# Adding u back without TensorE for 22 more token groups: VectorE transposes, a DRAM round trip and an add

## The chip, the cores and the metric

One core of a Trainium2 chip runs the whole program. The metric is the device time of one execution in microseconds; lower is better.

## The reference

The input is `x` of 8 batches, 3136 tokens and 256 channels. First a global filter along the tokens, by FFT; then a low-rank token mixer; then an MLP over the channels with a residual:

```
X = rfft(x, axis=1);  Y = X * (filt_r + 1j*filt_i);  y = irfft(Y)
h = (y^T @ U) @ V                 # U: 3136 x 32, V: 32 x 3136
u = y + h^T
out = u + relu(u @ w_ch1) @ w_ch2 # 256 -> 1024 -> 256
```

The output is float32; the kernel computes in float16 with float32 accumulation.

## The kernel before, in words

The 3136 tokens of a batch are taken as 49 x 64, and the transforms are matmuls with constant matrices. For each batch there are five stages, each a Python generator that issues a piece of its work at each `next`:

- `f1` (or `f1_turned` for batches 0 and 1): the first transform. `load_x` brings `x` in four blocks per batch, issued on GpSimd's queue (line 128). TensorE multiplies (L250), ScalarE copies the result into a tile with the tag `asb` (L255), and SyncE's queue stores it to DRAM (L257, L258).
- `mid`: loads what `f1` stored into `a2` tiles (L331, SyncE's queue; one load of 512 KB covers eight frequencies), second transform `pz` (L384, TensorE), product with the filter on VectorE (`uv`, L392, L396, L397), back transform `pe` (L345), a copy by ScalarE, and a store to DRAM (`ct2`, L364, SyncE's queue). A batch has 13 items of this kind; `pe` of an item comes three items later.
- `load_e2` reads `ct2` back into the rows of `eb` (L416), in three parts and two halves of 32 columns, 256 KB each.
- `rank`: the low-rank term (L423 and on), written into rows of `eb` by VectorE (L438).
- `s4`: the last transform (`pu`, L456), 16 items, the first eight from the first half of `eb`, copied by VectorE and ScalarE into `ut`. `ut` holds u with channels on the partitions.

The MLP works on 49 groups of 512 tokens, eight steps to a group: step t of group n issues `mm1` for it (L488, ReLU by ScalarE L491 into `h16`) and `mm2` for group n-1 (L544). `mm2` puts tokens on the partitions, so u must be turned before it can be added. There are two ways:

- `residual`: two matmuls with the identity for each 128 tokens (L536) add u to the accumulator `pc` in PSUM; VectorE then copies `pc` to `och` (L556). A group has eight such matmuls, in four pairs.
- `turn_u`, for groups from `FIRST_TURNED` = 37 on: two VectorE transposes of 32 x 32 blocks (L515) into a tile `tu`, four stores of 64 KB to DRAM (L520) and one load of 256 KB into `tur` (L524), both on SyncE's queue; VectorE then adds `pc` and `tur` into `och` (L552). The generator has four pieces: first transpose, second transpose, stores, load.

Every half group (steps t = 3 and t = 7 of `mm2`) ends in such a copy or add; at t = 7 GpSimd's queue issues the output of 512 KB (L561).

The order of the work is written out by hand: `plan[s]` lists which generators are advanced at the end of step s, of 392 steps. `S[b]` is the step at which the first group that reaches into batch b starts (0, 48, 96, 144, 192, 240, 288, 336). In the loop over b, `a` = S[b-1], `z` = S[b], and `e` = z-20 (z-17 for b = 1, z-22 for b = 6 and 7): `mid` of batch b is dealt over the steps from a-5 to e, its loads follow at e-5, e-4 and e+1, `rank` from e, `s4` from e+8 to z-2; at the same time `x` of batch b+1 is loaded and `f1` of it is dealt from a+10 to z-20 (a+21 to z-13 for b = 1). In those steps the MLP is working on batch b-1. Each engine, and each DMA queue, takes its instructions in this order and waits where its data or its buffer is not ready. A transfer that waits for a buffer holds up all that stand behind it on the same queue.

Of the kernel before, what the change touches and what calls it, by code (L numbers as in the profile page):

```python
# [10 lines left out]
F16 = mybir.dt.float16  # L11
# [7 lines left out]
DM = 256  # L19
# [3 lines left out]
NG = NB * SEQ // GT  # L23
FIRST_TURNED = 37
# [56 lines left out]
def kernel(  # L81
# [27 lines left out]
    sb = ctx.enter_context(tc.tile_pool(name="sb", bufs=1))  # L109
    ps = ctx.enter_context(tc.tile_pool(name="ps", bufs=2, space=bass.MemoryType.PSUM))  # L110

    def bank(tag, name, dtype=F32):

        return ps.tile([128, 512 if dtype == F32 else 1024], dtype, tag=tag, bufs=4 if tag == "z" else 2, name=name)

    def dram(t, off, dims):
        return bass.AP(tensor=t, offset=off, ap=[list(d) for d in dims])
# [5 lines left out]
    xt = {}  # L123

    def load_x(b, c):
        t = sb.tile([98, 8 * DM], F16, tag="x", bufs=4, name="x")
        for a, n in ((0, 96), (96, 2)) if b == 0 else ((0, 98),):
            nc.gpsimd.dma_start(t[a:a + n], dram(x.tensor, (b * SEQ + 8 * c + 32 * a) * DM, [[32 * DM, n], [1, 8 * DM]]))
        xt[b, c] = t
# [10 lines left out]
    for c in range(4):  # L140
        load_x(0, c)
# [64 lines left out]
    tu = eb[0:RANK, 0:12, :].rearrange("p r d -> p (r d)")  # L206
# [34 lines left out]
    def f1(b):  # L241
        for c in range(4):
            t = xt[b, c].rearrange("p (j d) -> p j d", d=DM)
            asb = sb.tile([98, 8, DM], F16, tag="asb", bufs=4, name="asb")
            for half in range(2):
                for i in range(2):
                    pf = bank("z", "pf")
                    for s in range(2):
                        j = 4 * half + 2 * i + s
                        nc.tensor.matmul(pf[0:98, 256 * s:256 * s + 256],  # L250
                                         ws[:, (8 * c + j) * 98:(8 * c + j + 1) * 98], t[:, j, :],
                                         start=(s == 0), stop=True, skip_group_check=True)
                    dst = asb[:, 4 * half + 2 * i:4 * half + 2 * i + 2, :]
                    src = pf[0:98].rearrange("p (j d) -> p j d", d=DM)
                    nc.scalar.copy(dst, src)  # L255
                    if half and i:
                        nc.sync.dma_start(dram(ct1[b], 8 * c * 96 * DM, [[DM, 96], [96 * DM, 8], [1, DM]]), asb[0:96])  # L257
                        nc.sync.dma_start(dram(ct0[b], 8 * c * DM, [[32 * DM, 2], [1, 8 * DM]]),  # L258
                                          asb[96:98].rearrange("p j d -> p (j d)"))
                    yield  # L260
# [151 lines left out]
    def load_e2(b, part, hs=(0, 1)):  # L412

        n = 12 if (b, part) == (0, 2) else 16
        for h in hs:
            nc.sync.dma_start(eb[32 + part:32 + 4 * n:4, 32 * h:32 * h + 32, :].rearrange("p (q r) d -> p q (r d)", r=8),  # L416
                              dram(ct2[b][part], 8 * h * DM, [[NR * DM, n], [16 * DM, 4], [1, 8 * DM]]))
# [61 lines left out]
    groups = [Group(n) for n in range(NG)]  # L479

    def utv(b):
        return ut[b].rearrange("p h q r -> p h (q r)")
# [11 lines left out]


    def turned(gr):
        return gr.n >= FIRST_TURNED

    def turn_u(gr):

        t = sb.tile([128, 4, 4, 2, 32], F16, tag="asb", bufs=4, name="tu")
        for dh in range(2):
            for b, t0, o, n in gr.seg:
                j, z = o // 32, (o + n) // 32
                while j < z:

                    k = min(z, j + 4 - j % 4) if j % 4 or z - j < 4 else z - z % 4
                    src = utv(b)[:, dh, t0 + 32 * j - o:t0 + 32 * k - o]
                    if k - j < 4:
                        dst = t[:, j % 4:j % 4 + k - j, j // 4, dh, :]  # L510
                        src = src.rearrange("p (c e) -> p c e", e=32)
                    else:
                        dst = t[:, :, j // 4:k // 4, dh, :].rearrange("p c g e -> p g c e")
                        src = src.rearrange("p (g c e) -> p g c e", c=4, e=32)
                    nc.vector.transpose(dst, src)  # L515
                    j = k
            yield
        td = nc.dram_tensor(f"tu_{gr.n}", (128, 4 * DM), F16, kind="Internal")
        for a in range(4):
            nc.sync.dma_start(dram(td, DM * a, [[4 * DM, 32], [128 * DM, 4], [1, DM]]),  # L520
                              t[32 * a:32 * a + 32].rearrange("i c g h e -> i c (g h e)"))
        yield
        gr.tu = sb.tile([128, 4, 4, 2, 32], F16, tag="x", bufs=4, name="tur")
        nc.sync.dma_start(gr.tu.rearrange("p a g h e -> p (a g h e)"), td.ap())  # L524
        yield

# [11 lines left out]
    def mm2(gr, t):  # L538
        i, half = t // 2, t % 2
        if t % 4 == 0:  # L540
            gr.pc = bank("o", "pc")
        o = gr.pc[:, 256 * (i % 2):256 * (i % 2) + 256]
        for tt in range(4 * half, 4 * half + 4):
            nc.tensor.matmul(o, gr.h[tt][:, 128 * i:128 * i + 128], w2sb[:, tt, :],  # L544
                             start=(tt == 0), stop=(tt == 7 and turned(gr)), skip_group_check=True)
        if half and not turned(gr):
            residual(gr, o, i)
        if t % 4 == 3:
            if t == 3:
                gr.och = sb.tile([128, 4, DM], F32, tag="och", bufs=2, name="och")  # L550
            if turned(gr):
                nc.vector.tensor_add(gr.och[:, i - 1:i + 1, :].rearrange("p g (h a e) -> p (g h) a e", h=2, a=4),  # L552
                                     gr.pc.rearrange("p (f a e) -> p f a e", f=4, a=4),
                                     gr.tu[:, :, i - 1:i + 1].rearrange("p a g h e -> p (g h) a e"))
            else:
                nc.vector.tensor_copy(gr.och[:, i - 1:i + 1, :], gr.pc.rearrange("p (j d) -> p j d", d=DM))  # L556
            if gr.n == NG - 1:
                nc.sync.dma_start(dram(out.tensor, (gr.n * GT + 128 * (i - 1)) * DM, [[DM, 128], [128 * DM, 2], [1, DM]]),
                                  gr.och[:, i - 1:i + 1, :])
            elif t == 7:  # L560
                nc.gpsimd.dma_start(dram(out.tensor, gr.n * GT * DM, [[DM, 128], [128 * DM, 4], [1, DM]]), gr.och)  # L561
# [3 lines left out]
    plan = [[] for _ in range(8 * NG)]  # L565

    def deal(gen, count, a, z):
        for i in range(count):
            plan[max(0, int(a + i * (z - a) / count))].append(gen)

    def later_x(b, c):
        load_x(b, c)
        yield

    f1s = [f1(b) if b > 1 else f1_turned(b) for b in range(NB)]
    mids = [mid(0, "o")] + [mid(b) for b in range(1, NB)]
    ranks = [rank(b) for b in range(NB)]
    s4s = [s4(b) for b in range(NB)]
    turns = [turn_u(gr) for gr in groups]

    u_hat()
# [4 lines left out]
    for i in range(16):  # L586
# [3 lines left out]
        next(f1s[0])  # L590
    nc.gpsimd.dma_start(sv[32:97], sv_d.rearrange("k (r q) -> k r q", q=NQ))
    load_x(1, 0)
    nc.gpsimd.dma_start(w1sb, moe_w_ch1.rearrange("(h dd) c -> dd h c", h=2))
    spread_filters(2)
# [29 lines left out]
    for _ in s4s[0]:  # L624
        pass

    def loads(b, part):
        load_e2(b, part)
        yield

    for b in range(1, NB):
        a, z = S[b - 1], S[b]
        e = z - (17 if b == 1 else 20 if b < 6 else 22)
        deal(mids[b], 13, a + {1: 8, 2: -3}.get(b, -5), e - 4)
        deal(mids[b], 4, e - 4, e)
        for p, at in enumerate((e - 5, e - 4, e + 1)):
            plan[at].append(loads(b, p))
        deal(ranks[b], 6, e, e + 6)
        deal(s4s[b], 16, e + 8, z - 2)
        if b == 1:  # L640
            deal(f1s[1], 12, 1, 8)
        if b + 1 < NB:
            for c in range(4):
                plan[a + (9 + 2 * c if b == 1 else 1 + 4 * c)].append(later_x(b + 1, c))
            deal(f1s[b + 1], 16, a + (21 if b == 1 else 10), z - (13 if b == 1 else 20))

    for gr in groups:
        if turned(gr):
            for i in range(4):
                plan[8 * gr.n + (0, 1, 2, 5)[i]].append(turns[gr.n])  # L650
    for n, gr in enumerate(groups):
        for t in range(8):
            mm1(gr, t)
# [36 lines left out]
```

## Time and profile before

| what | value |
|---|---|
| three runs | 517.74, 514.62, 516.92 us; median 516.92 |
| the profiled execution | 516.43 us, of which the span of the program is 514.6 us |
| TensorE busy | 490.5 us (95%), granted clock 0.995 |
| VectorE / ScalarE / GpSimd busy | 366.2 / 377.1 / 80.6 us |
| moved by DMA | 94.52 MB |
| L536, matmuls with the identity | 302 |
| L515, transposes on VectorE | 28 |

A line of the groups in the profile reads: source line, engine, operation, result and sources, shape, count, then busy time and mean duration of one in nanoseconds, then the idle time of the engine just before these instructions and what ended it. A line of the order of time reads: start and length in microseconds, engine, line, operation, and in brackets the idle time before it with its releaser. A line of a stretch gives the busy time of TensorE, of its weight loads, of VectorE, ScalarE and GpSimd, then the granted clock, the busy share of the DMA engines and the GB/s.

### The profile page before, as it was taken

The numbers are of one execution on the slowest core, as the hardware profiler recorded it, in microseconds if no ns is written. First come the engines' busy times: TensorE is split into PE (matmuls) and PEld (weight loads), VectorE is DVE, ScalarE is ACT, GpSimd is POOL, SyncE is SP. The second block draws the span as 40 slices with busy tenths as digits, with TensorE's granted clock in tenths as the row PEclk, the third lists the DMA queues.
The fourth block names the chain that finished last, engine by engine and source line by source line (L and its number), as shares of the span: only waits on it lengthen the run. The fifth ranks groups of instructions, "written<-read, shape, count | busy, mean of one in ns | idle before, by whom it ended". The sixth has DMA issues, their size and how long they took to land.

```text
span 514.6 us, 11909 instructions
## 1 busy us (share of the span) xinstructions
PE 490.5 (95%) x4754; PEld 349.6 (68%) x4754; DVE 366.2 (71%) x497; ACT 377.1 (73%) x704; POOL 80.6 (16%) x122
## 2 busy tenths in 40 slices
PE   3887899999999999999999999999999998999996
PEld 3645566776767777777767777777677765676665
DVE  5886599579847986679747986679846997853332
ACT  6874778867986689667986689667886676666663
POOL 6662010002001110002001110002001000011110
PEclk9998999999999999999999999999999999999999
DMA  8987926957877286837877286837877136644454
GB/s 187 175 206 174 181 74 172 281 171 176 216 229 251 69 186 190 298 130 177 213 227 254 69 185 202 262 156 184 218 228 240 65 126 206 212 153 149 126 162 163
DMA packets 76016, 94.52 MB, mean 184 GB/s; under 512 B 5795, under 2 KB 58979, under 8 KB 75960
## 3 DMA queue, kind: packets, MB, share of 16 engines
q1 hardware_dynamic: 61256, 52.17, 33.9%
q0 software_dynamic: 14704, 41.58, 31.4%
q8 instruction: 37, 0.61, 0.5%
q14 instruction: 19, 0.16, 0.1%
HBM read 58.35 MB, written 50.92 MB: 212 GB/s over the span
## 4 chain that ended last, share of the span: by engine, by line
PE 81%; DVE 8%; DMA 4%; issue 1%; ACT 1%; SPq 0%; POOL 0%; DVEq 0%; POOLq 0%
PE pc L544 31%; PE phh L488 30%; DVE uv L392 5%; PE pu L456 5%; PE pf L250 4%; PE pe L345 4%; PE pz L384 3%; PE pc L536 3%; DMA w2sb<-in_moe_w_ch_dram 2%; PE ph L423 1%; DVE uv L397 1%; DMA eb<-ct 1%; DVE uv L396 1%; DMA ct<-e 1%; DVE och L556 1%
## 5 line engine op out<-in xcount | busy, mean ns | idle before, releaser
L491 ACT ACTIVATE h<-phh 128x512 f16<-128x512 f32 x392 | 235.9, 603 | 83.2 <-PE phh L488 81.7
L544 PE MATMUL pc<-w2sb,h 128*128 128x256 f16 x1568 | 233.7, 272 | 1.2 <-DMA w2sb<-in_moe_w_ch_dram 1.2
L488 PE MATMUL phh<-ut,w1sb 128*128 128x512 f16 (+7 forms) x896 | 233.3, 352 | 0.4 <-DVE ut L463 0.4
L544 PEld LDWEIGHTS <-h 128*128 128x128 f16 x1568 | 151.7, 97 | 91.8 <-issue 1.5
L392 DVE TENSOR_TENSOR uv<-pz,fab 128x1024 f16<-128x1024 f32 (+1 forms) x104 | 120.6, 1177 | 12.5 <-PE pz L384 10.5
L561 POOL DMA_DIRECT2D out_dram<-och x48 | 39.1, 814 | 402.0 <-DVE och L556 318.8
L488 PEld LDWEIGHTS <-w1sb 128*128 128x128 f16 x896 | 78.9, 97 | 19.8 <-issue 1.5
L556 DVE COPY och<-pc 128x512 f32<-128x512 f32 x74 | 51.0, 689 | 44.4 <-PE pc L536 43.5
L355 ACT CAST e<-pe 128x512 f16<-128x512 f32 x96 | 56.6, 591 | 21.0 <-PE pe L345 20.2
L463 DVE CAST ut<-pu 128x392 f16<-128x392 f32 x92 | 48.5, 557 | 17.9 <-PE pu L456 16.0
L255 ACT CAST asb<-pf 98x512 f16<-98x512 f32 x96 | 57.3, 599 | 0.2
L438 DVE COPY eb<-h 32x4096 f16<-32x4096 f16 x32 | 38.2, 1232 | 14.2 <-ACT h L435 14.2
L552 DVE TENSOR_TENSOR och<-pc,tur 128x512 f32<-128x512 f32 x24 | 16.5, 689 | 39.8 <-PE pc L544 37.3
L345 PE MATMUL pe<-uv,m 128*128 128x512 f16 (+1 forms) x117 | 41.3, 371 | 3.6 <-DVE uv L392 1.5
L456 PE MATMUL pu<-sv,eb 97*128 97x49 f16 x1024 | 40.5, 187 | 3.3 <-DMA eb<-ct 3.1
L456 PEld LDWEIGHTS <-eb 97*128 97x128 f16 x1024 | 37.7, 98 | 4.8 <-DVE eb L438 3.4
L536 PE MATMUL pc<-idn,ut 128*128 128x128 f16 (+1 forms) x302 | 40.8, 219 | 0.0
L384 PE MATMUL pz<-a,m 128*128 128x512 f16 x96 | 36.2, 379 | 1.1 <-DVE a L311 1.0
L250 PE MATMUL pf<-x,ws 98*98 98x256 f16 x192 | 36.6, 273 | 0.0
L396 DVE TENSOR_TENSOR uv<-uv 64x1024 f16<-64x1024 f16 (+1 forms) x49 | 30.9, 630 | 1.7
L536 PEld LDWEIGHTS <-ut 128*128 128x128 f16 (+1 forms) x302 | 28.8, 98 | 3.9 <-issue 0.6
L397 DVE TENSOR_TENSOR uv<-uv 64x1024 f16<-64x1024 f16 (+1 forms) x49 | 30.7, 627 | 0.7
(80 smaller groups left out, 264.9 us busy)
## 6 DMA issues: line engine op xcount, KB each, us to landing
out_dram<-och POOLq DMA_DIRECT2D x48, 512.0 KB, 4.4
ct<-e SPq DMA_DIRECT2D x47, 256.0 KB
eb<-ct SPq DMA_DIRECT2D x46, 256.0 KB
x<-in_x_dram POOLq DMA_DIRECT2D x28, 392.0 KB, 7.8
ct<-asb SPq DMA_DIRECT2D x24, 384.0 KB
a<-ct SPq DMA_DIRECT2D x18, 512.0 KB
tu<-tu SPq DMA_DIRECT2D x48, 64.0 KB
tur<-tu SPq DMA_DIRECT2D x12, 256.0 KB
```

Source lines behind the costliest of these rows:

```text
L250: nc.tensor.matmul(pf[0:98, 256 * s:256 * s + 256], ws[:, (8 * c + j) * 98:(8 * c + j + 1) * 98], t[:, j, :], start=(s == 0), stop=True, s ...
L255: nc.scalar.copy(dst, src)
L345: nc.tensor.matmul(pe[:, 0:n], w, uv[:, f, o:o + n], start=(f == 0), stop=(b > 0 or f == 1))
L355: nc.scalar.copy(t[:, 2 * (i % 2):2 * (i % 2) + 2, :].rearrange("p k d -> p (k d)"), pe)
L384: nc.tensor.matmul(pz, a2m, src[:, k:k + 2, :].rearrange("p k d -> p (k d)"), start=True, stop=True)
L392: nc.vector.tensor_mul(uv[:, :, o:o + n], zin, fin)
L456: nc.tensor.matmul(pu[:, NQ * i:NQ * i + NQ], eb[:, 8 * n + i, d], sv[:, 8 * g + i, :], start=(i == 0), stop=True, skip_group_check=True)
L488: nc.tensor.matmul(ph[:, o:o + n], w1sb[:, dh, 128 * t:128 * t + 128], utv(b)[:, dh, t0:t0 + n], start=(dh == 0), stop=(dh == 1), skip_gro ...
L491: nc.scalar.activation(h, ph, RELU)
L536: nc.tensor.matmul(d, w, idn, start=False, stop=(dh == 1), skip_group_check=True)
L544: nc.tensor.matmul(o, gr.h[tt][:, 128 * i:128 * i + 128], w2sb[:, tt, :], start=(tt == 0), stop=(tt == 7 and turned(gr)), skip_group_check ...
L556: nc.vector.tensor_copy(gr.och[:, i - 1:i + 1, :], gr.pc.rearrange("p (j d) -> p j d", d=DM))
```

## The change

The last four groups of each of the batches 1 to 5 (two of batch 0), counted from 0 as the batches in the MLP, take the second way too: the groups 4 and 5, 8 to 11, 14 to 17, 20 to 23, 26 to 29 and 32 to 35. Their pieces are put at steps of their own relative to z and e. `tu` and `tur` get two buffers of their own instead of sharing those of `asb` and `x`, which go from four to three each. Three of the first eight `x` blocks are put in `asb` buffers. The fourth `x` block of a batch is loaded five steps later (twelve for batch 2). The rows of `eb` are loaded half by half: the first halves at e-5, e-4 and e+1, the second halves of all three parts at e+2.

```diff
     def load_x(b, c):
-        t = sb.tile([98, 8 * DM], F16, tag="x", bufs=4, name="x")
+        tag = "asb" if (b, c) in ((0, 3), (1, 0), (1, 1)) else "x"
+        t = sb.tile([98, 8 * DM], F16, tag=tag, bufs=3, name="x")
...
-            asb = sb.tile([98, 8, DM], F16, tag="asb", bufs=4, name="asb")
+            asb = sb.tile([98, 8, DM], F16, tag="asb", bufs=3, name="asb")
...
     def turned(gr):
-        return gr.n >= FIRST_TURNED
+        return gr.n >= FIRST_TURNED or gr.n in turn_at
...
-        t = sb.tile([128, 4, 4, 2, 32], F16, tag="asb", bufs=4, name="tu")
+        t = sb.tile([128, 4, 4, 2, 32], F16, tag="tu", bufs=2, name="tu")
...
-        gr.tu = sb.tile([128, 4, 4, 2, 32], F16, tag="x", bufs=4, name="tur")
+        gr.tu = sb.tile([128, 4, 4, 2, 32], F16, tag="tur", bufs=2, name="tur")
...
-    def loads(b, part):
-        load_e2(b, part)
+    def loads(b, parts, h):
+        for part in parts:
+            load_e2(b, part, [h])
         yield
+    turn_at = {n: [8 * n + i for i in (0, 1, 2, 5)] for n in range(FIRST_TURNED, NG)}
...
-        for p, at in enumerate((e - 5, e - 4, e + 1)):
-            plan[at].append(loads(b, p))
+        for at, parts, h in ((e - 5, [0], 0), (e - 4, [1], 0), (e + 1, [2], 0), (e + 2, range(3), 1)):
+            plan[at].append(loads(b, parts, h))
+        if z < 8 * FIRST_TURNED:
+            if b > 1:
+                turn_at[z // 8 - 4] = [z - 37, z - 35, z - 33, z - 29]
+                turn_at[z // 8 - 3] = [z - 31, z - 29, z - 27, z - 23]
+            turn_at[z // 8 - 2] = [e - 3, e - 2, e + 3, e + 7]
+            turn_at[z // 8 - 1] = [e - 1, e, e + 5, z - 8]
...
-                plan[a + (9 + 2 * c if b == 1 else 1 + 4 * c)].append(later_x(b + 1, c))
+                plan[a + (9 + 2 * c + 12 * (c > 2) if b == 1 else 1 + 4 * c + 5 * (c > 2))].append(later_x(b + 1, c))
...
-    for gr in groups:
-        if turned(gr):
-            for i in range(4):
-                plan[8 * gr.n + (0, 1, 2, 5)[i]].append(turns[gr.n])
+    for n, at in turn_at.items():
+        for i in at:
+            plan[i].append(turns[n])
```

## The prediction

> **What bounds the kernel now.** I read the page first, then TensorE's waits, then TensorE, VectorE and SyncE in order of time at one batch boundary (batch 3 to 4), then stretches.
>
> ```profile
> span 514.6 us, 11909 instructions
> PE 490.5 (95%) x4754; PEld 349.6 (68%) x4754; DVE 366.2 (71%) x497; ACT 377.1 (73%) x704; POOL 80.6 (16%) x122
> PE   3887899999999999999999999999999998999996
> DVE  5886599579847986679747986679846997853332
> DMA  8987926957877286837877286837877136644454
> L536 PE MATMUL pc<-idn,ut 128*128 128x128 f16 (+1 forms) x302 | 40.8, 219 | 0.0
> ```
>
> TensorE has a 9 in every slice from 64 us to 424 us, and after 60 us its waits for other work come to 2.5 us in all. So time on TensorE is time of the kernel, unless taking work off it starves it. The loss would come from VectorE, which is full in some slices and half idle in others, or from the transfers, which go in bursts.
>
> **Part 1: the residual matmuls removed.** `turned` becomes true for 22 more groups: 4 and 5 of batch 0, then the last four of each of batches 1 to 5 (8-11, 14-17, 20-23, 26-29, 32-35; groups that straddle two batches stay). Each loses 4 pairs of L536. Matmuls overlap, so the 219 ns is not their price; the distance between starts is:
>
> ```profile
> 220.27 0.27 PE L536 MATMUL pc<-idn,ut 128*128 128x128 f16 x2
> 220.38 0.58 PE L456 MATMUL pu<-sv,eb 97*128 97x49 f16 x16
> ...
> 225.75 0.38 PE L384 MATMUL pz<-a,m 128*128 128x512 f16 x1
> ```
>
> A pair holds TensorE from 220.27 to 220.38, 0.11 us. 22 groups x 4 pairs x 0.11 = **9.7 us off**. The order of the built program shows it: 352 fewer rows on TensorE, 176 weight loads and 176 matmuls.
>
> **Part 2: VectorE's new work.** Each group adds two transposes and turns two copies into adds.
>
> ```profile
> L515 DVE STREAM_TRANSPOSE tu<-ut 128x512 f16<-128x512 f16 x22 | 14.5, 688 | 0.1
> L552 DVE TENSOR_TENSOR och<-pc,tur 128x512 f32<-128x512 f32 x24 | 16.5, 689 | 39.8 <-PE pc L544 37.3 <-DMA tur<-tu 2.5
> L556 DVE COPY och<-pc 128x512 f32<-128x512 f32 x74 | 51.0, 689 | 44.4 <-PE pc L536 43.5
> ```
>
> Add and copy cost the same 689 ns. The transposes are 44 x 0.69 = 30 us, hidden where VectorE has idle time. The first four of a batch (steps z-37, z-35, z-31, z-29) fall, in batch 4's `mid`, into about 246 to 257 us:
>
> ```profile
> 246.00:250.00 4.00, 4.00 (x34) 2.98 (x33) 2.88 (x4) 3.69 (x8) 0.00 (x0) 1.00 0.96 182
> 250.00:254.00 4.00, 4.00 (x30) 2.68 (x29) 3.05 (x4) 3.68 (x8) 0.79 (x1) 1.00 0.78 232
> 254.00:258.00 4.00, 4.00 (x32) 2.92 (x31) 3.32 (x5) 3.49 (x8) 0.00 (x0) 1.00 0.79 243
> ```
>
> VectorE's column (the third engine) leaves 1.12 + 0.95 + 0.68 = 2.75 us; four transposes take 2.75. It just fits, and the next 4 us hold 1.07 more. The other four (around e) fall into 262 to 270 us, where it is idle 6.1 of 8. Batch 6 has less room: 2.0 us idle in 362 to 374, so 0.8 us of lag reaches the end of its `mid`. If the cover is gone, the price has a precedent in batch 7, where two turned groups already meet a `mid`:
>
> ```profile
> 432.12 0.39 PE L345 MATMUL pe<-uv,m 128*128 128x512 f16 x1 [1.33 <-DVE uv L397]
> ```
>
> So the bounds are 0 and 1.3 us in each of five `mid`s, 0 to 6.5. I take 0.4 in all, half of batch 6's lag: four of five stretches fit.
>
> **Part 3: SyncE's queue, and what waits in it.** Each group adds four stores of 64 KB and one load of 256 KB, 22 x 0.52 = 11.5 MB. Per batch 2.1 MB; in the tail, where only such stores, loads and the output move, 20 us carry 3.2 MB at a busy share of 0.49, 3.1 us per MB, so a batch gains 6.5 us of transfer in its 58 us: room on average (share about 0.7), not in every burst. The added wait that matters is the last group's `tur` load, at step z-8. `tur` has two buffers, so this load waits for the second add of the group two before, at step z-9. Queued behind it on SyncE are the loads of `a2` for the next `mid` (L331), which TensorE needs at step z-5. Before, they went out early:
>
> ```profile
> 212.78 1.16 SPq L416 DMA_DIRECT2D eb<-ct  x2
> 214.04 0.54 SPq L331 DMA_DIRECT2D a<-ct  x1
> ...
> 220.58 0.69 DVE L556 COPY och<-pc 128x512 f32<-128x512 f32 x1 [0.42 <-PE pc L536]
> ```
>
> They leave at 214.04, 11.7 us before the matmul at 225.75. Afterwards they leave when the add that stands where this copy stands has ended, 221.27. From there to 225.75 is 4.48 us (163.50 to 168.0 and 279.30 to 283.8 in other batches: the same), less two removed pairs, 4.26. In it a `tur` load (256 KB) and the first `a2` load (512 KB) must land. The nearest row is the last `tur` load:
>
> ```profile
> 506.45 0.34 SPq L524 DMA_DIRECT2D tur<-tu  x1
> ...
> 509.11 0.69 DVE L552 TENSOR_TENSOR och<-pc,tur 128x512 f32<-128x512 f32 x1 [1.34 <-DMA tur<-tu]
> ```
>
> 2.66 us from issue to use on quiet queues. 512 KB more at the 293 GB/s of 213 to 222 us, or at peaks of 380, are 1.8 or 1.4 us: 4.1 to 4.5 us. The group's output (512 KB, other queue) leaves at the same moment and can put up to 1.8 us between. So a stall of 0 to 2.0 us per boundary; I take 0.6, the output costing a third of its bytes. Boundaries where this happens: into batches 3 to 7, five (group 5's load finds a fresh buffer). **Plus 3.0 us**, bounds 0 and 10.
>
> The Trainium skill gives another price: DMA: Bandwidth & Descriptors, section Anatomy of one DMA, fits a transfer on the GpSimd path as 2.0 us plus its bytes at 436 GB/s. The 2.66 us of the 256 KB load agree with its 2.6; by it the 768 KB would take 3.8 us, as an estimate, less than the 4.26 allowed, and the stall would be nothing. The same page (section Rules for kernel authors) says that below 64 KB a transfer is mostly overhead; the four 64 KB stores stand at that edge, and no run here shows one large store instead.
>
> **Part 4: the rest.** (a) Row loads by halves: the same six transfers per batch; the later halves follow 0.6 us apart from 213 us, 1 MB and an output at 293 GB/s land by about 219, and the first use is the ninth `s4` item at 222.86. Nothing. In batch 7 two of these loads now stand ahead of group 39's `tur` load, whose add already waited 1.13 us at 446.30; 1.2 us of issue more, of which I count 0.4 (bounds 0 and 2). (b) The fourth `x` load goes out behind the output at step a+15, about 193.3 in batch 4's loading, and is needed at 201.93. The first `x` load behind an output landed after 5.7 to 6.3 us, a second one after up to 9.1: I take 0, bounds 0 and 0.5 in each of five. Batch 2's is needed at 95.14 and leaves at 87.3. (c) Three asb buffers: `f1`'s fourth block meets a store issued 11 us before. 0. (d) The prologue's x loads wait less; TensorE's wait there for the second weight was 1.2 us, so 0, bounds -1.2 and +1.2.
>
> **Sum.** The profiled execution took 516.43 (span 514.6 and 1.8 around it), 0.5 below the median of 516.92. 516.43 - 9.7 + 0.4 + 3.0 + 0.4 = 510.5; from the median 511.0. I predict **510.8**. The terms' ends give 505.5 and 528; as not all go one way, the forecast's own range is 508 to 513.5.
>
> **Rivals.**
> *No stall at all.* The `a2` loads land in time; 516.4 - 9.7 = 506.7. For it: the quiet landing lies at the limit and 222 to 226 us show a transfer share of only 0.36. Against: that stretch now holds what was moved there. The skill's fit ends here.
> *VectorE becomes the bound.* Every one of the five `mid`s pays batch 7's 1.3 us and the boundary still pays: 510.5 + 6 = 516. For it: 2.75 us of work into 2.75 us of gaps. Against: after its `mid` VectorE has a gap of 4 us and more in each batch, and TensorE uses a product three items later.
> *`a2` loads much too late: slower.* One mechanism: SyncE held at the `tur` load, then the first `a2` load landing like an `x` load on busy queues, 7.8 us instead of the 3.9 left after its issue: 3.9 x 5 = 19.5 on top of 506.7 is 526. It ends slower than before once a landing takes more than 5.8 us. For it: eight stores and four row loads stand ahead on the queue, and the last of them may hold SyncE beyond the add. Against: the queue drained at 300 to 380 GB/s there.
> That the edit does not do what it says is excluded by the 176 missing matmuls.
>
> **Numbers.** Forecast 0.44, no stall 0.24, VectorE 0.15, late loads 0.17. A measurement tells 1%, about 5.2 us, from nothing: 511.75 is the border. Of the forecast 0.32 lies below it, 0.12 above; no stall is faster; VectorE same; of late loads 0.15 slower, 0.02 same. Faster 0.56, same 0.29, slower 0.15. Range: 506 to 521, leaving out about 0.05 below and 0.15 above.
>
> **What would show it.** Right: L536 at 126 matmuls; TensorE's waits name a `pz` matmul waiting for an `a2` load five times, about 0.6 us each; the `a2` loads issued within 1 us of the add at z-9; transposes 72 in all, and VectorE busy about 396 us. Wrong: `pe` waiting for VectorE in every `mid` (the VectorE rival), `pf` waiting for `x` (then part 4b was mis-sized), or `pz` waits of several us (late loads); no waits and 507 would say that my landing price was too high.

## The result, and the profile after

The changed kernel is slower: a median of 540.5 us (533.0 to 547.7, six runs) against 516.0 (514.4 to 519.0) of the kernel before on the same chip, a ratio of **1.037 [1.033, 1.041]**. The profiled execution took 542.6 us and is one of the longer ones, while the ratio rests on the shorter ones (533 to 538); readings of single waits below are therefore on the high side by some us in all. Line numbers of the changed kernel are higher by 2 than those of before (`pz` L386, `pu` L458, `turn_u` L517 to L526, `residual` L538, `mm2` L546, add L554).

The page of the changed kernel, its span, its engines, and three of its rows in 40 slices:

```profile
span 540.9 us, 11742 instructions
PE 490.7 (91%) x4578; PEld 343.2 (63%) x4578; DVE 392.0 (72%) x541; ACT 375.8 (69%) x704; POOL 80.8 (15%) x122
PE   4887899979997899799999899889999798999996
PEclk9998999979999899989999999989999899999999
DMA  9987727948798387885897588976897435834444
```

TensorE executes 176 matmuls less and is still busy for 490.7 us. Its row, which was 9 everywhere from 64 to 424 us, has dents at every batch boundary, and the row of the granted clock has dents in the same slices or the next at five of the six. (A boundary here is the stretch in which `mid` of one batch ends, its `s4` begins with `pu`, and `mid` of the next begins with `pz`; it is named by the z of the loop over b, 48 to 288.)

Its groups by line, those that the change touches:

```profile
L554 DVE TENSOR_TENSOR och<-pc,tur 128x512 f32<-128x512 f32 x68 | 46.8, 689 | 64.8 <-PE pc L546 55.8 <-DMA tur<-tu 7.9
L517 DVE STREAM_TRANSPOSE tu<-ut 128x512 f16<-128x512 f16 (+2 forms) x72 | 45.8, 662 | 4.7 <-DMA tu<-tu 4.2
L538 PE MATMUL pc<-idn,ut 128*128 128x128 f16 (+1 forms) x126 | 16.6, 220 | 0.0
```

126 matmuls with the identity are left, and VectorE does 72 transposes and 68 adds: the edit does what it says.

TensorE's waits (engine, result, line, what it waited for; us in total, times, longest):

```profile
PE pz L386 <- DMA a<-ct: 11.8, 5, 3.4
PE pu L458 <- DMA eb<-ct: 9.2, 4, 3.4
...
PE pu L458 <- issue: 3.5, 2, 3.3
PE pu L458 <- DVE ut L465: 2.7, 2, 1.6
PE pe L347 <- DVE uv L399: 1.5, 1, 1.5
```

Two loads cost most: `a2` of the next `mid`, and `eb`, the rows for `s4`. Of the 9.2 us for `eb`, one wait of 3.4 us ends at 43.9 us, in the prologue, where the kernel before has the like of it:

```profile
PE pu L456 <- DMA eb<-ct: 3.1, 1, 3.1
```

At the boundaries `eb` costs 5.8 us under its name. The 3.3 us under "issue" are read as a wait for `eb` as well: at the boundary at z = 144 `pu` starts 3.33 us after the loads of `eb` leave, and where the trace names the wait it was 3.9, 3.9 and 4.1 us. ScalarE's copy of the last `mid` item at that boundary, SyncE's queue, and the two matmuls, in three views:

```profile
217.25 0.63 ACT L357 CAST e<-pe 128x512 f16<-128x512 f32 x1
```

```profile
220.32 0.34 SPq L526 DMA_DIRECT2D tur<-tu  x1
220.71 0.51 SPq L366 DMA_DIRECT2D ct<-e  x1
...
226.87 2.44 SPq L418 DMA_DIRECT2D eb<-ct  x4
229.41 4.45 SPq L522 DMA_DIRECT2D tu<-tu  x8
234.47 2.02 SPq L526 DMA_DIRECT2D tur<-tu  x2
236.56 0.42 SPq L333 DMA_DIRECT2D a<-ct  x1
```

```profile
230.20 0.82 PE L458 MATMUL pu<-sv,eb 97*128 97x49 f16 x16 [3.26 <-issue]
...
241.56 0.39 PE L386 MATMUL pz<-a,m 128*128 128x512 f16 x1 [1.02 <-DVE ut L465]
```

The copy has ended at 217.88. The store of its result (`ct2`) leaves 2.83 us later, because a `tur` load stands ahead of it and waits for its own four stores. That is the common case: from 60 to 430 us SyncE's queue stood 21.8 us at such loads (L526) for their stores, and 3.2 us for an add.

```profile
SPq L526 <- DMA tu<-tu: 21.8, 17, 4.3
SPq L526 <- DVE och L554: 3.2, 3, 2.0
```

The store lands at 226.87, when the loads of `eb` leave; 3.33 us later the first of them lets `pu` start. Behind `eb` SyncE issues eight stores for 4.45 us, then two `tur` loads, then `a2` at 236.56. The other boundaries look alike, with the delay divided between `pu` and `pz` in other parts: 1.6 + 2.4, 2.2 + 3.4, 3.3 + 1.0, 1.0 + 2.1, 2.6 + 0.8 and 0 + 3.2 us (z = 48, 96, 144, 192, 240, 288), 23.5 in all. Two of these, the 1.6 at z = 48 and the 1.0 at z = 144, the trace puts down to VectorE's copy of `pu` (L465) and not to a load.

At five of the six boundaries a second loss follows. Stretches of the changed kernel around a `pz` wait that ends at 177.99 (TensorE, weight loads, VectorE, ScalarE, GpSimd, then granted clock, DMA share, GB/s):

```profile
174.00:178.00 4.00, 0.60 (x13) 0.46 (x11) 1.16 (x2) 0.62 (x2) 0.00 (x0) 1.00 1.00 355
178.00:180.00 2.00, 2.00 (x22) 1.45 (x23) 1.27 (x2) 0.60 (x1) 0.00 (x0) 0.69 0.43 174
180.00:182.00 2.00, 2.00 (x19) 1.20 (x16) 0.99 (x2) 0.60 (x1) 0.00 (x0) 0.50 0.00 0
182.00:184.00 2.00, 2.00 (x20) 1.33 (x18) 1.42 (x2) 1.18 (x3) 0.00 (x0) 0.96 0.00 0
```

While TensorE is idle, the DMA engines are full (share 1.00); when the data is there, TensorE soon runs at half its clock, for 3.41 us (178.76 to 182.17). There are five such spells after 60 us, one of them twice as long; the kernel before has none there:

```profile
113.91:120.74 6.83, 5.40 (x20) 2.74 (x21) 2.62 (x4) 1.20 (x3) 0.35 (x1) 0.50 0.43 155
178.76:182.17 3.41, 3.41 (x36) 2.42 (x34) 1.92 (x3) 1.20 (x2) 0.00 (x0) 0.50 0.05 19
229.96:233.37 3.41, 3.17 (x39) 2.35 (x40) 1.31 (x3) 0.60 (x1) 0.00 (x0) 0.50 0.92 279
352.84:356.25 3.41, 3.41 (x32) 2.00 (x29) 1.58 (x3) 1.08 (x2) 0.00 (x0) 0.50 0.77 231
424.52:427.93 3.41, 3.41 (x27) 2.13 (x26) 1.68 (x2) 1.19 (x2) 0.00 (x0) 0.50 0.25 101
```

TensorE worked 18.8 us in them, which costs 9.4 us.

### The profile page after: what moved, and what is told of

Its sections match the earlier page's. It is cut to its first block, busy times and chain, and to the rows that moved or that the text cites. A ratio compares the mean times of both kernels' runs of the same rounds, so it can differ in the third digit from the quotient of the medians.

```text
span 540.9 us, 11742 instructions
## 1 busy us (share of the span) xinstructions
PE 490.7 (91%) x4578; PEld 343.2 (63%) x4578; DVE 392.0 (72%) x541; ACT 375.8 (69%) x704; POOL 80.8 (15%) x122
## 4 chain that ended last, share of the span: by engine, by line
PE 56%; DMA 22%; issue 10%; DVE 6%; ACT 2%; POOL 2%; SPq 1%; POOLq 0%; DVEq 0%
PE pc L546 21%; PE phh L490 21%; DMA x<-in_x_dram 6%; DMA ct<-e 6%; DMA a<-ct 5%; PE pu L458 4%; DVE uv L394 3%; DMA eb<-ct 3%; PE pf L252 3%; PE pe L347 2%; PE pz L386 2%; DMA tur<-tu 1%; POOL x L130 1%; SPq L418 1%; ACT e L357 1%
## 5 line engine op out<-in xcount | busy, mean ns | idle before, releaser
L546 PE MATMUL pc<-w2sb,h 128*128 128x256 f16 x1568 | 237.5, 276 | 0.8 <-DMA w2sb<-in_moe_w_ch_dram 0.8
L490 PE MATMUL phh<-ut,w1sb 128*128 128x512 f16 (+7 forms) x896 | 237.1, 357 | 0.4 <-DVE ut L465 0.4
L546 PEld LDWEIGHTS <-h 128*128 128x128 f16 x1568 | 153.5, 99 | 94.9 <-issue 5.8
L554 DVE TENSOR_TENSOR och<-pc,tur 128x512 f32<-128x512 f32 x68 | 46.8, 689 | 64.8 <-PE pc L546 55.8
L490 PEld LDWEIGHTS <-w1sb 128*128 128x128 f16 x896 | 80.6, 98 | 20.7 <-issue 2.1
L357 ACT CAST e<-pe 128x512 f16<-128x512 f32 x96 | 56.6, 591 | 18.7 <-PE pe L347 18.0
L465 DVE CAST ut<-pu 128x392 f16<-128x392 f32 x92 | 48.3, 559 | 28.1 <-PE pu L458 25.8
L458 PE MATMUL pu<-sv,eb 97*128 97x49 f16 x1024 | 42.2, 190 | 15.5 <-DMA eb<-ct 9.2
L458 PEld LDWEIGHTS <-eb 97*128 97x128 f16 x1024 | 40.3, 100 | 19.6 <-issue 10.4
L386 PE MATMUL pz<-a,m 128*128 128x512 f16 x96 | 36.8, 385 | 14.3 <-DMA a<-ct 11.8
L517 DVE STREAM_TRANSPOSE tu<-ut 128x512 f16<-128x512 f16 (+2 forms) x72 | 45.8, 662 | 4.7 <-DMA tu<-tu 4.2
L399 DVE TENSOR_TENSOR uv<-uv 64x1024 f16<-64x1024 f16 (+1 forms) x49 | 30.7, 627 | 0.7
L252 PEld LDWEIGHTS <-ws 98*98 98x98 f16 x192 | 22.4, 125 | 10.7 <-DMA x<-in_x_dram 1.4
L463 ACT CAST ut<-pu 128x392 f16<-128x392 f32 x36 | 17.5, 486 | 13.7 <-PE pu L458 8.7
```

The costliest lines, as they stand in the source:

```text
L252: nc.tensor.matmul(pf[0:98, 256 * s:256 * s + 256], ws[:, (8 * c + j) * 98:(8 * c + j + 1) * 98], t[:, j, :], start=(s == 0), stop=True, s ...
L357: nc.scalar.copy(t[:, 2 * (i % 2):2 * (i % 2) + 2, :].rearrange("p k d -> p (k d)"), pe)
L386: nc.tensor.matmul(pz, a2m, src[:, k:k + 2, :].rearrange("p k d -> p (k d)"), start=True, stop=True)
L458: nc.tensor.matmul(pu[:, NQ * i:NQ * i + NQ], eb[:, 8 * n + i, d], sv[:, 8 * g + i, :], start=(i == 0), stop=True, skip_group_check=True)
L465: nc.vector.tensor_copy(dst, src)
L490: nc.tensor.matmul(ph[:, o:o + n], w1sb[:, dh, 128 * t:128 * t + 128], utv(b)[:, dh, t0:t0 + n], start=(dh == 0), stop=(dh == 1), skip_gro ...
```

## The experiments

All ratios are against the kernel before, run on the same chip beside each; experiments are edits of the changed kernel unless it is said otherwise.

**1. The terms of the sum: no transfers, and no turned groups**

`e4_no_transfers` turns the same groups by the same VectorE instructions, but has neither the stores nor the loads; the old turned groups of the tail lose theirs too:

```diff
-        t = sb.tile([128, 4, 4, 2, 32], F16, tag="tu", bufs=2, name="tu")
+        t = sb.tile([128, 4, 4, 2, 32], F16, tag="tu", bufs=4, name="tu")
...
-        td = nc.dram_tensor(f"tu_{gr.n}", (128, 4 * DM), F16, kind="Internal")
-        for a in range(4):
-            nc.sync.dma_start(dram(td, DM * a, [[4 * DM, 32], [128 * DM, 4], [1, DM]]),
-                              t[32 * a:32 * a + 32].rearrange("i c g h e -> i c (g h e)"))
...
-        gr.tu = sb.tile([128, 4, 4, 2, 32], F16, tag="tur", bufs=2, name="tur")
-        nc.sync.dma_start(gr.tu.rearrange("p a g h e -> p (a g h e)"), td.ap())
+        gr.tu = t
```

> The turned groups keep their transposes and adds on VectorE, but the round trip through DRAM is left out and the add takes the half-turned tile, so out is not u + ch there. Theories Q and B: the loss is in the transfers, and what is left is the 9.7 us taken off TensorE; 505 to 509 us (a little under that, as the old turned groups lose their transfers too). Theory V: 530 us or more, as VectorE's work is unchanged.

Measured: 505.4 us, ratio 0.980 [0.976, 0.983]. From its page:

```profile
PE 480.4 (96%) x4578; PEld 339.4 (68%) x4578; DVE 391.1 (78%) x541; ACT 375.9 (75%) x704; POOL 80.5 (16%) x122
PEclk9998999999999999999999999999999999999999
```

The same 4578 TensorE instructions take 480.4 us, 10.1 less than before and 10.3 less than in the changed kernel; VectorE's 391.1 us are hidden. All of the loss comes with the transfers.

`e6_rest_alone` keeps the halves, the moved `x` load and the buffers, and turns no further group:

```diff
-        if z < 8 * FIRST_TURNED:
+        if False:
```

> The rest of the change alone: buffers, x order, loads by halves and the new tiles for the last twelve groups, no new turned groups. Both theories (and part 4 of the prediction): within 1% of the kernel before, 514 to 518 us. If 525 or more, the loss would lie in the rest and not in the new transfers.

Measured: 516.5 us, ratio 1.001 [0.998, 1.003]. The rest costs nothing that the runs can tell from noise.

**2. Which transfers: stores, loads, or both**

Three kernels in which the add reads a resident constant, so that nothing waits for the round trip. `e7_bytes_no_waits` has all stores, and loads of the same size from a constant in DRAM; `e9_stores_alone` has the stores only, `e10_loads_alone` the loads only.

```diff
-        gr.tu = sb.tile([128, 4, 4, 2, 32], F16, tag="tur", bufs=2, name="tur")
-        nc.sync.dma_start(gr.tu.rearrange("p a g h e -> p (a g h e)"), td.ap())
+        r = sb.tile([128, 4, 4, 2, 32], F16, tag="tur", bufs=2, name="tur")
+        nc.sync.dma_start(r.rearrange("p a g h e -> p (a g h e)"), dram(ws_d.tensor, 0, [[1024, 128], [1, 1024]]))
+        gr.tu = fab[:, 0, 0:4, :].rearrange("p a (g h e) -> p a g h e", g=4, h=2)
```

> The changed kernel with every store and load of the turned groups, but the load fetches a constant and the add takes a resident constant, so no load waits for its stores, no load waits for an add, and no add waits for a load; out is not u + ch there. Theory Q: the loss is in these waits, 506 to 514 us. Theory B: the bytes are the same, pu still waits for eb; 525 us or more. Between: both have a share.

> As the run with bytes and no waits, but the loads back are left out: the stores alone, 5.8 MB in pieces of 512 bytes (out is not u + ch in the turned groups). Theory B in the form that bytes count: half of the loss comes back, 514 to 521 us. In the form that the small pieces count: little comes back, 522 us or more. Theory Q (what is left of it, the number of transfers that SyncE issues ahead of the a2 loads): eight stores still stand ahead of them, pz waits over 8 us.

> The same with the loads alone and no stores: 5.8 MB in pieces of 2 KB, one transfer per group instead of five (out is not u + ch in the turned groups). Bytes count: 514 to 521 us. Small pieces count: 505 to 511 us. Number of transfers on SyncE counts: 505 to 511 us as well, with pz waits under 2 us.

Measured: both 530.0 us, 1.020 [1.012, 1.029]; stores alone 509.2, 0.988 [0.983, 0.993]; loads alone 507.7, 0.986 [0.981, 0.991]. Over `e4`'s 0.980 the stores cost 0.85% (4.4 us), the loads 0.64% (3.3 us), both together 4.1% (21 us). The stretch from the first `x` load of a batch to the first `pz` at z-5 for z = 144, of before, `e4`, `e10`, `e9` and `e7`, in that order:

```profile
175.50:225.80 50.30, 50.30 (x489) 36.45 (x487) 35.49 (x47) 40.28 (x76) 6.44 (x10) 1.00 0.77 223
```

```profile
171.70:220.10 48.40, 48.40 (x460) 34.64 (x458) 39.84 (x55) 39.59 (x76) 6.38 (x9) 1.00 0.81 232
```

```profile
173.20:221.70 48.50, 48.50 (x461) 34.72 (x459) 39.95 (x55) 39.72 (x76) 6.47 (x10) 1.00 0.86 245
```

```profile
174.70:225.00 50.30, 48.71 (x461) 34.78 (x458) 41.06 (x56) 39.87 (x76) 6.45 (x10) 1.00 0.87 232
```

```profile
179.30:232.20 52.90, 49.00 (x461) 34.89 (x460) 41.17 (x56) 40.06 (x76) 6.47 (x10) 1.00 0.88 241
```

Length times DMA share is the time that the transfers take: 39.2 us in `e4`, 41.7 with the loads, 43.8 with the stores, 46.6 with both. The DMA time adds up (2.5 + 4.6 = 7.1, measured 7.4), but the lost time does not. The extra transfers are nearly hidden when they add 2.5 or 4.6 us to this stretch; with 7.4 us more, in a stretch that has room for 48.4 x 0.19 = 9.2 us on paper, they are not. So the price is far from a sum of its parts (21 us, with an interval of some 4 us to either side, against 7.7), and most of it is paid even where no transfer waits for the round trip. The shares of the lengthened stretches, 0.87 and 0.88, do not tell these cases apart.

**3. Which groups**

`e8_last_two_only` drops the first two groups of each batch (and loads the last `tur` at z-2); `e11_first_two_only` drops the last two. First the edit of `e8`, then that of `e11`:

```diff
-            if b > 1:
-                turn_at[z // 8 - 4] = [z - 37, z - 35, z - 33, z - 29]
-                turn_at[z // 8 - 3] = [z - 31, z - 29, z - 27, z - 23]
```

```diff
-            turn_at[z // 8 - 2] = [e - 3, e - 2, e + 3, e + 7]
-            turn_at[z // 8 - 1] = [e - 1, e, e + 5, z - 8]
```

> Only the last two groups of each batch are turned in addition (12 groups instead of 22), and the last load is at z-2 as in the run with the last load later. No new transfer then stands ahead of the last ct2 store. Theories Q and B both: pu waits for eb under 3 us in all, pz for a2 under 2; 12 x 4 x 0.11 = 5.3 us off, 510 to 513 us. If it stays over 520, the late transfers cost by themselves.

> Only the first two groups of the four (10 groups, batches 1 to 5) are turned in addition; nothing new stands between the eb loads and the a2 loads. Theory B: their transfers fall into the stretch in which the DMA engines are already full before the last ct2 store, so pu still waits for eb, 8 us or more, pz for a2 under 2 us; 518 to 526 us, slower than before in spite of 4.4 us less on TensorE. If it is under 513 us, these transfers do no harm alone and only all four groups together do.

Measured: the last two 514.1 us, 0.994 [0.991, 0.997]; the first two 525.6, 1.017 [1.011, 1.022]. TensorE's waits of the second:

```profile
PE pu L458 <- DMA eb<-ct: 9.9, 4, 3.3
```

2.1 us of this are the prologue's; 7.8 are at the boundaries, with 0.8 more under "issue", against 5.8 and 3.5 in the changed kernel. So the first two groups alone make nearly the whole `eb` wait, and no `pz` wait. The last two make no new wait at the boundaries after 115 us.

**4. Which wait in SyncE's queue**

`e1_last_load_later` puts the last `tur` load behind the `a2` loads; `e2_third_load_later` puts the load at z-23 behind the last `ct2` store; `e3_both_later` does both.

```diff
-            turn_at[z // 8 - 1] = [e - 1, e, e + 5, z - 8]
+            turn_at[z // 8 - 1] = [e - 1, e, e + 5, z - 2]
```

```diff
-                turn_at[z // 8 - 3] = [z - 31, z - 29, z - 27, z - 23]
+                turn_at[z // 8 - 3] = [z - 31, z - 29, z - 27, e + 2]
```

> The load back of each batch's last turned group goes from step z-8 to z-2, behind the a2 loads in SyncE's queue. Theory Q (the order of SyncE's queue: waits of the turned groups' transfers hold up the a2 loads and, earlier, the last store of ct2): the waits of pz for a2 (11.8 us in the changed kernel) fall under 3 us, the waits of pu for eb stay at about 9 us; about 522 us. Theory B (the added 11.5 MB fill the DMA engines, the order does not matter): pz still waits over 8 us; 530 us or more. Theory V (VectorE is the bound): no change, 533 us or more.

> The load back of each batch's second turned group goes from step z-23 to e+2, behind the last ct2 store and the eb loads. Theory Q: that store leaves within 1 us of ScalarE's copy, the waits of pu for eb fall from about 13 us (9.2 named, 3.5 unnamed) to under 5, those of pz for a2 stay; about 522 us. Theory B: both stay, 530 us or more. Theory V: 533 us or more.

> Both loads moved, all bytes still moved. Theory Q: most of TensorE's idle time at the boundaries goes, and with it the stretches of lower clock; 507 to 513 us. Theory B: over 525 us. Theory V: 530 us or more.

Measured: `e1` 529.2 us, 1.026 [1.020, 1.032]; `e2` 544.9, 1.048 [1.041, 1.056]; `e3` 534.4, 1.036 [1.032, 1.040]. In `e1` the `pz` waits for `a2` fell from 11.8 us to one of 0.4, and those of `pu` stayed (3.7 of the first line are the prologue's, so 6.7 and 3.8 at the boundaries):

```profile
PE pu L458 <- DMA eb<-ct: 10.4, 5, 3.7
...
PE pu L458 <- issue: 3.8, 1, 3.8
```

So the place of the last `tur` load makes `pz` wait, and is worth about 1% of the 3.7%; part of the delay only moved to `pu`, which comes first. `e2` shows that the held-up store is not cured by moving one load: `tur` of that group is then late for its add (VectorE waits 28.7 us for `tur`, against 7.9, and `pu` 9.3 us for VectorE), and the queue is held up by the `tur` load of the group before instead, so that the store at z = 144 still leaves 1.7 us late. In `e3` no `pz` waits for a load any more, but `pu` waits 11.5 us for VectorE.

**5. Another queue**

`e5_pool_queue` issues all transfers of the turned groups on GpSimd's queue; `e13_two_queues` those of the first two groups only, with their stores and loads some steps later, and the last load at z-2. `e14_two_queues_20` is `e13` without the groups 4 and 5. The edits of `e5` and of `e13`:

```diff
-            nc.sync.dma_start(dram(td, DM * a, [[4 * DM, 32], [128 * DM, 4], [1, DM]]),
+            nc.gpsimd.dma_start(dram(td, DM * a, [[4 * DM, 32], [128 * DM, 4], [1, DM]]),
...
-        nc.sync.dma_start(gr.tu.rearrange("p a g h e -> p (a g h e)"), td.ap())
+        nc.gpsimd.dma_start(gr.tu.rearrange("p a g h e -> p (a g h e)"), td.ap())
```

```diff
+        q = nc.gpsimd if gr.n in on_pool else nc.sync
...
-                turn_at[z // 8 - 4] = [z - 37, z - 35, z - 33, z - 29]
-                turn_at[z // 8 - 3] = [z - 31, z - 29, z - 27, z - 23]
+                turn_at[z // 8 - 4] = [z - 37, z - 35, z - 30, z - 26]
+                turn_at[z // 8 - 3] = [z - 31, z - 29, z - 25, z - 19]
+                on_pool.update((z // 8 - 4, z // 8 - 3))
```

> All transfers of the turned groups, stores and loads, are issued on GpSimd's queue instead of SyncE's; steps, bytes and waits as in the changed kernel. Theory Q: SyncE's queue is as free as before, the last ct2 store leaves within 1 us of ScalarE's copy, pu and pz wait under 3 us each; about 508 to 515 us, unless the waits now hold up the x loads and the outputs, which stand in that queue. Theory B: the bytes are the same, pu and pz wait as in the changed kernel, 530 us or more.

> All 22 groups and all bytes, in two queues: the first two groups of each batch on GpSimd's queue, behind the fourth x load (stores at z-30 and z-25, loads at z-26 and z-19), the last two on SyncE's with the last load at z-2. Theory B in the form that the engines have no time left for these bytes: pu or pf still waits for transfers, 15 us and more together, 522 us or more. Theory F (the bytes fit, but a queue hands over its transfers in the order of issue, so each of the added ones delays the ct2 store, the eb loads and the a2 loads that stand behind it): pu under 4 us, pz under 2, pf under 4 in all; 507 to 514 us.

> The same without groups 4 and 5 (20 groups): 0.9 us more on TensorE, and the waits at 112 us of the other kernels (pu for VectorE, pz for a2, 1 to 3 us) gone. Theory F: 507 to 513 us, within 2 us of the run with 22 groups. Theory B: 520 us or more.

Measured: 531.7 us, 1.027 [1.021, 1.034]; 527.1, 1.023 [1.018, 1.027]; 527.9, 1.024 [1.021, 1.028]. In `e5` SyncE is free of them, `pz` waits for no load, and the `x` loads that stand behind the waiting transfers on GpSimd's queue are late in their stead:

```profile
PE pf L252 <- DMA x<-in_x_dram: 10.4, 6, 2.4
```

In `e14` the last `ct2` store leaves 0.02 us after the copy and still lands only 5.7 us later, with a DMA share of 1.00 in between; `eb` then leaves as late as before (5.8), not later. What remains in `e14` is `a2`, which still stands behind the eight stores of the last two groups (5.6 us of `pz` waits), and VectorE, which now waits 13.5 us for `tur` (4.2 us of `pu` waits). So another queue moves the delay as well. The Trainium skill (DMA: Bandwidth & Descriptors, section Issuing engines are not separate DMA queues) says that transfers from all engines end on the same 16 DMA engines. These runs are in line with it, but as each has waits of its own they do not prove it.

**6. Fewer bytes at the same place**

`e15_less_output` does not write the output of two groups per batch that leaves between the `x` loads and the loads of `eb`, one ahead of the last `ct2` store and one just behind it; `e16_less_output_last_load_later` adds the edit of `e1`.

```diff
+    no_out = {8 * (b * SEQ // GT) // 8 - i for b in range(2, 7) for i in (5, 4)}
...
-            elif t == 7:
+            elif t == 7 and gr.n not in no_out:
```

> The changed kernel with all its new transfers, steps and waits, but the output of two groups per batch (10 groups, 512 KB each, on GpSimd's queue) is not written: two outputs that fall between the x loads and the eb loads. Theory B (the engines are full in this stretch, whoever issues): 1 MB less there takes back the 1 MB of the first two groups' round trip, and pu's waits for eb go; 512 to 522 us. Theory F (order in SyncE's queue alone): nothing of what stands in that queue is changed, 528 us or more.

> Both remedies at once: two outputs per batch not written (which left pu 2.5 us of waits for eb, but pz 16.3 for a2) and the load back of the last group at z-2 (which left pz under 1, but pu 14). If the loss is two causes, full engines ahead of the eb loads and the a2 loads behind a waiting load in SyncE's queue, each hiding part of the other: both waits gone, 506 to 514 us. If the engines are simply full everywhere, the waits come back elsewhere: 520 us or more.

Measured: 535.9 us, 1.041 [1.038, 1.044]; 526.3, 1.022 [1.018, 1.025]. The waits of `e15`:

```profile
PE pz L386 <- DMA a<-ct: 16.3, 6, 3.8
...
PE pu L458 <- DMA eb<-ct: 2.5, 4, 0.9
```

With 1 MB less per boundary the wait for `eb` at the boundaries shrinks from 9.3 us (with "issue") to 2.9, and `pz` takes over the delay. Either remedy moves the delay, and both together still leave 526 us.

**7. The boundary at z = 144 in nine of them**

From the traces in the order of time, in us after the end of ScalarE's copy of the last `mid` item (so 217.88 is 0 for the changed kernel), with the wait in brackets:

| kernel | `ct2` store leaves | lands: `eb` leaves | `a2` leaves | `pu` starts | `pz` starts |
|---|---|---|---|---|---|
| before | 0.1 | 5.8 | 7.1 | 9.6 | 18.8 |
| no transfers (`e4`) | 0.0 | 3.5 | 6.9 | 8.9 | 17.7 |
| loads alone (`e10`) | 0.1 | 4.7 | 8.8 | 8.9 | 17.7 |
| stores alone (`e9`) | 0.0 | 4.7 | 13.5 | 8.9 | 19.4 [1.6] |
| last two groups (`e8`) | 0.0 | 3.5 | 12.8 | 9.6 | 18.6 |
| first two groups (`e11`) | 1.8 | 7.4 | 10.0 | 10.7 [1.7] | 19.7 |
| both, no waits (`e7`) | 1.2 | 6.0 | 14.5 | 9.5 [0.5] | 21.9 [3.4] |
| less output, load later (`e16`) | 1.3 | 7.0 | 14.5 | 9.9 [0.9] | 20.8 [2.0] |
| changed kernel | 2.8 | 9.0 | 18.7 | 12.3 [3.3] | 23.7 [1.0] |

This is the mechanism as this boundary shows it, row by row. There is one chain, copy, `ct2` store, `eb` loads, `pu`, and one behind it on the same queue, `eb`, stores of the last two groups, `a2`, `pz`. As estimates from these traces: `pu` needs `eb` to leave by about 8.9 - 3.3 = 5.6; `a2` took 6.0 to 7.4 us to land where `pz` waited for it here (`e9`, `e16`, `e7`), so it must leave by about 10.3 to 11.7. The stores and loads of the first two groups make the `ct2` store leave late and land late; the eight stores of the last two hold SyncE for 4 to 6 us between `eb` and `a2`. With one of the two, each deadline is met or missed by up to 1.7 us (in `e11` by 2.8 and 3.3 at two other boundaries); with both, the delays add up on one queue and both deadlines are missed.

**8. A version that beats both**

The kernel before, with the last two groups of batches 1 to 5 turned, the last load at z-2, its own buffers, `x` loads and row loads unchanged:

The steps of all turned groups stand in `turn_at`, as in the changed kernel.

```diff
...
+        if b > 1 and z < 8 * FIRST_TURNED:
+            turn_at[z // 8 - 2] = [e - 3, e - 2, e + 3, e + 7]
+            turn_at[z // 8 - 1] = [e - 1, e, e + 5, z - 2]
```

> The kernel before (four x and four asb buffers, loads in one, x at the old steps) with the last two groups of batches 1 to 5 turned in addition (10 groups), the last load at z-2. 10 x 4 x 0.11 = 4.4 us off TensorE and no waits of pu, pz or pf after 100 us: 511 to 513 us. Over 515 if the transfers after the eb loads cost by themselves.

Measured: 511.4 us (511.1 to 512.3), 0.991 [0.988, 0.994]. Ten groups at 4 pairs of 0.11 us are 4.4 us, and 4.0 were gained.

## Why the prediction was wrong, step by step

The forecast was 510.8 us in a range of 506 to 521; the ratio puts the time at 533 to 538, and the result lies outside.

- **Part 1, 9.7 us of residual matmuls: right.** TensorE's work fell by 10.1 us (`e4` against before), 126 matmuls are left, and without transfers the kernel takes 505.4 us where "no stall at all" gave 506.7. A part of the 1.3 us between may be the tail, whose old round trips `e4` drops too.
- **Part 2, VectorE: right.** Busy for 392 us (396 forecast), no `mid` waits for it; `pe` waits for L399 once, as before, in batch 7 (1.5 us). The rival in which VectorE becomes the bound is out by `e4`.
- **Part 3, the transfers: the step that failed.** The term was +3.0 us with bounds of 0 and 10. Between `e4` and the changed kernel lie 5.7% of 516, 29 us. Four things in it were wrong:
  1. A chain without slack was not priced. The prediction followed only what stands behind the load at z-8, the `a2` loads, and let that load wait for an add alone. But the load at z-23 stands ahead of the last `ct2` store and waits for its own stores, and in the profile of before the chain from that store over `eb` to `pu` (207.01, 212.78, 216.51) just fitted: `eb` had 3.73 us to land, and in the changed kernel, where it was waited for, it took 3.3 to 4.1. No wait was shown there, and none was looked for, because a chain that just fits leaves no line among the waits. At the boundaries it came to 5.8 us, and 3.5 more under "issue".
  2. The landing of `a2` was priced at 4.1 to 4.5 us, from the quiet tail and a mean rate. From issue to `pz` it took 6.9, at most 5.0, 4.0, 4.8 and 6.2 us at the five boundaries; in the 2 us before `pz` the DMA share was 0.93 to 1.01. The order of events was right, with `a2` leaving 0.44 us after the add at z = 144; at the five forecast boundaries `pz` waited 3.4, 1.0, 2.1, 0.8 and 3.2 us, 2.1 on average and not 0.6, and 2.4 us at z = 48, where no wait was forecast. The Trainium skill's fit (DMA: Bandwidth & Descriptors, section Anatomy of one DMA) is for the GpSimd path; the estimate of 3.8 us from it for the two loads would have put the stall at nothing, and the `a2` load alone took longer here.
  3. "Room on average" was taken over the whole 58 us of a batch. In before, the share is 0.77 from the `x` loads to `pz`, and the idle time lies behind `pz`, where the transfers of this change cannot use it. In the changed kernel the share is 0.89 to 1.06 in every 2 us from 216 to 226, just where the `ct2` store must land. The kernel before was as full there, but for a shorter time. From the copy to the `eb` loads, before and changed kernel:

```profile
206.95:212.78 5.83, 5.83 (x65) 4.01 (x63) 2.54 (x4) 4.18 (x9) 0.00 (x0) 1.00 0.95 324
217.88:226.87 8.99, 8.99 (x82) 5.83 (x79) 7.19 (x8) 6.62 (x14) 1.15 (x1) 1.00 0.96 292
```

  4. A stall was priced by its length alone. TensorE was busy for 490.7 us with work that takes 480.4 at full clock: 10.3 us were lost to the granted clock after the stalls (9.4 of them in the five spells at half clock), a term that was missing altogether.
- **The sum, in the profiled executions**, as an account of busy and idle time: 514.6 - 10.1 (work) + 10.3 (clock) + 26.1 (idle time of TensorE: 50.2 against 24.1) = 540.9.
- **Part 4, the rest: right.** 1.001 by `e6`. `x` made `pf` wait once after 75 us, 1.0 us at 276 us.
- **The rival of `a2` loads much too late, 526 us,** had the side, the queue and the wait, but not the price: `pz` waited 11.8 us for `a2`, not 19.5, and the rest of the loss came from `eb` (9.3) and the clock (10.3), which no rival held.
- **Small slips of the working.** The upper ends of its terms add up to 528.9, not 528; nothing hangs on it.

What stays open: at the boundary the delay is partly order on SyncE's queue and partly full DMA engines. `e1`, `e5` and `e14` show that neither alone explains it, and how the 526 us of `e16` divide was not separated. Stores of the last two groups placed behind the `a2` loads were not tried, and the table in time was made for one boundary only.

## What to carry to other kernels

Work taken off the engine that sets the time was priced to 0.4 us; what it was traded for must be followed chain by chain, also through places where the profile of before shows no wait, by measuring how late each transfer could have landed. Read the DMA share in the stretch in which the new transfers must move, not over the loop, and expect that the price may rise steeply where two nearly harmless additions meet (4.4 and 3.3 us alone, 21 together). Take the part of the change that fits the slack: ten groups gained 0.9% where 22 lost 3.7%.

## What the hardware showed that was not expected

- After a wait of 3.4 us (end at 177.99) TensorE was granted half its clock for 3.41 us. The Trainium skill (TensorE: Matmul & The Clock Gate, section Part 1: The HAM clock gate (the "warmup" mystery)) tells of half the clock after an idle window of about 3.4 us, until about 3.4 us of work. The trace agrees in the 0.50 and the 3.41 us, but shorter waits do the same: in `e16` one of 1.95 us, ending at 230.60, was followed by 0.50, while in the changed kernel one of 2.06 us, ending at 302.43, was followed by no fall. The starts of the five spells of the changed kernel lie 19, 15, 36 and 21 times 3.413 us apart, so they stand on a fixed raster, a row of equal stretches of that length. Stretches of this raster, `e16` first, then the changed kernel:

```profile
228.62:232.03 3.41, 1.46 (x21) 1.04 (x21) 2.03 (x3) 0.59 (x2) 0.00 (x0) 1.00 1.00 397
232.03:235.45 3.42, 3.42 (x28) 1.79 (x24) 1.78 (x4) 1.17 (x3) 0.00 (x0) 0.50 0.22 83
...
298.23:301.64 3.41, 2.15 (x36) 1.65 (x33) 2.21 (x5) 1.68 (x3) 0.00 (x0) 1.00 1.01 377
301.64:305.05 3.41, 2.62 (x38) 1.94 (x39) 2.34 (x4) 1.01 (x2) 0.00 (x0) 1.00 0.84 294
```

  The wait of `e16` falls into one stretch (1.95 us idle); the longer one is cut in two (1.26 and 0.79). In the 18 traces of this case, from 60 to 495 us, each of the 33 stretches at full clock with more than 1.8 us idle was followed by half the clock, and none of the 2202 with less than 1.75 us. So here it was the idle time in a stretch of the raster that counted, from about half of it on, and not the length of one wait.

- 1 MB of stores of 64 KB took 4.6 us of DMA time in the stretch, the same bytes as loads of 256 KB 2.5 us (`e9` and `e10` over `e4`), and each such store held SyncE for 0.50 to 0.73 us (eight behind `eb` took 4.0 to 5.8 us at the six boundaries of the changed kernel).
